# Attention and feed-forward on one core: stage tiles 2080 bytes apart in SBUF instead of 2048

## The chip, the core and the metric

The kernel runs on one NeuronCore of a Trainium2 chip, as one launch. The metric is the device time of that launch in microseconds (us). Engines are named as in the profile: PE is TensorE (PEld its weight loads), DVE is VectorE, ACT is ScalarE, POOL is GpSimd, SP the engine whose queue issues all DMAs.

## The reference

Local-window attention with global tokens, then a feed-forward layer with a leaky ReLU. Eight batches, eight heads, 512 local and 32 global tokens per head, 64 wide. A local token sees the 32 global keys and the local keys at most 32 places away; a global token sees all.

```python
s_g = scale * q_g @ concat(k_g, k_l).T ;  out_g = softmax(s_g) @ concat(v_g, v_l)
s_l = concat(scale * q_l @ k_g.T, where(|i-j| <= 32, scale * q_l @ k_l.T, -1e9))
out_l = softmax(s_l) @ concat(v_g, v_l)
x = concat(out_g, out_l) as [8*544 tokens, 512]
h = x @ w_in                                  # w_in 512 x 2048
g = max(h, 0) + alpha * min(h, 0)             # alpha per column of h
out = g @ w_out                               # w_out 2048 x 512, float32
```

## The kernel before

**Work and order.** The feed-forward layer fills most of the run. Its tokens form nine groups: eight batches of 512 local tokens, and one group of 256 global tokens. In each group a loop over f goes through 16 slices of 128 columns of w_in; one pass of it is called a step T, 144 in all. To keep float32 accuracy each factor is split into a high and a low part in the fp32r type: weights into w_hi and w_lo (tile `wt`), x into `xh` and `xl`, g into `gh` and `gl`. Three products are kept of four.

- `f1(T)` makes h for one slice in PSUM (`h_ps`): for each of four 128-row pieces of x three matmuls, w_hi·xh, w_lo·xh and w_hi·xl, with all tokens of the group (512, or 256 in the last group) as columns of the moving operand: 12 matmuls.
- `leak` (ACT, relu of -h), `bend` (DVE, g = beta·relu(-h) + h), `round_g` (ACT, `gh`), `rest_g` (`gl` = g - gh, on DVE for the first group and on POOL for the others) turn h into g.
- `f2(T - 2)` adds w_out·g to four PSUM banks `o`: eight matmuls with `gh` as moving operand, four with `gl`. After the last slice of a group the banks are copied out (`ost`) and written to HBM.

Every one of these matmuls has its own 128x128 weights, so PE issues one weight load per matmul; the next load runs under the current matmul.

The attention of the 32 pairs of heads is dealt out between these steps. Eight pairs and the decoding of the weights stand ahead in a hand-written order (`ORDER`); the others are planned at fixed steps: `local_scores` (`s_ps`, small matmuls on `qk`), `local_maxima` and `local_exps` (`p`), `local_exchange` (DVE transposes `p` into `pb`, which goes to HBM and comes back as `pt`), `local_values` (`o_ps`), `local_weights` (`xq`, exchanged through `xb` into `x_raw`), and the global tokens' parts (`g_ps`, `gt`, `go`, `gx`). All engine calls go through a recording layer, so DVE, ACT and SP instructions of the opening carry line 77, matmuls line 108, transposes on PE line 111, and `gl` on POOL line 464.

**Where the tiles lie.** SBUF tiles are placed one behind the other, rounded to 32 bytes per partition. The order that matters here: `alpha_sb` (with `PAD[0]` extra columns), `mask`, `ident`, `x_raw`, `x_glb`, `qk` (with `PAD[1]` extra columns), `vw` of the later pairs, small tiles, three wide tiles for the decoding, 21 stage tiles, small tiles, 17 weight tiles of 8192 bytes. The stage tiles hold everything of 512 columns that is short-lived, all under one tag:

```python
def stage(name, dtype=F32):
    return work.tile([128, 512], dtype, tag="st", name=name, bufs=NST)
```

So `xh`, `xl`, `g`, `gh`, `gl`, `p`, `pb`, `pt`, `xq`, `xb` and `ost` are stage tiles. In the built program the 21 of them start at byte 45056, 47104, ... 86016 of each partition, all multiples of 2048; the weight tiles start at 88576 + 8192 n, all multiples of 512. A 128x128 weight slice starts at a multiple of 512 in its tile. The distance from the moving operand of a feed-forward matmul to its weights is therefore a multiple of 512 for all 3456 of them. `x_raw` starts at 384 past a multiple of 512.

Of the kernel before, what the change touches and what calls it, by code (L numbers as in the profile page):

```python
# [27 lines left out]
NST = 21  # L28
# [2 lines left out]
TC = dict(schedule_with_timeline_sim=True)  # L31
HP = 50
HPU = 4
PAD = (32, 32)
LAG = 2
NRAW = 2 * NPAIR
ORDER = """
# [46 lines left out]
def longformer_ffn(ctx: ExitStack, tc: tile.TileContext, qk, vs, gn, vg, w, alpha, out):  # L84
# [5 lines left out]
    work = ctx.enter_context(tc.tile_pool(name="work", bufs=1))  # L90
# [3 lines left out]

    alpha_sb = const.tile([128, NF + PAD[0]], F32, name="alpha_sb")[:, 0:NF]
    mask = const.tile([128, 4, 128], F32, name="mask")
# [14 lines left out]
        return tc.keep_in_program_order(nc.tensor.transpose(*a))  # L111

    def stage(name, dtype=F32):
        return work.tile([128, 512], dtype, tag="st", name=name, bufs=NST)

    def small(name, n=4):
        return work.tile([128, n], F32, tag=name, name=name, bufs=4)
# [93 lines left out]
    def load_qk(P):  # L211
        if P < NPAIR:
            qks[P] = wpool.tile([128, 2048], F32, tag="w", name="qk")[:, 0 : SL + KS]
        else:
            qks[P] = work.tile([128, SL + KS + PAD[1]], F32, tag="qk", name="qk", bufs=1)[:, 0 : SL + KS]
        dma.dma_start(qks[P], qk[P])
# [31 lines left out]
    def local_maxima(P):  # L248
        for h in range(2):
            s, mn = ps_of[P, h], small("mn")  # L250
            if P < NRAW:
                src, scale = s.rearrange("q (i n) -> q i n", i=4), 0.125
                vec.tensor_reduce(mn, src, axis=AX.X, op=ALU.max)
                vec.tensor_scalar(mn, mn, -0.125, None, op0=ALU.mult)
            else:
                p = stage("p")
                src, scale = p.rearrange("q (i n) -> q i n", i=4), -1.0
                vec.scalar_tensor_tensor(p, s, -0.125, mask.rearrange("q i n -> q (i n)"), op0=ALU.mult, op1=ALU.add)
                vec.tensor_reduce(mn, src, axis=AX.X, op=ALU.min)
                pr_of[P, h] = p  # L260
            ps_of[P, h] = src, mn, scale

    def local_exps(P):
        z_of[P] = small("z", 8)
        for h in range(2):
            src, mn, scale = ps_of.pop((P, h))
            p = pr_of[P, h] = stage("p") if P < NRAW else pr_of[P, h]
            for i in range(4):
                k = 2 * i + h
                act.activation(p[:, 128 * i : 128 * i + 128], src[:, i], AF.Exp, bias=mn[:, i : i + 1], scale=scale, accum_out=z_of[P][:, k : k + 1])  # L270
        rz_of[P] = small("rz", 8)
        act.activation(rz_of[P], z_of.pop(P), AF.Copy, bias=1e-9)
# [9 lines left out]
    def local_copies(P):  # L282
        for h in range(2):
            pt_of[P, h] = stage("pt")
            copy("a" if P >= NPAIR or P in (3,) else "d", pt_of[P, h], ps_of.pop((P, h)))
# [368 lines left out]
```

## Time and profile before

| what | us |
|---|---|
| median of two timed runs | 916.97 (916.1 to 917.84) |
| the profiled execution, its own time | 917.19 |
| span of its instructions | 915.4 |
| PE busy (share of the span) | 890.9 (97%) |
| PEld busy | 718.8 (79%) |
| DVE, ACT, POOL busy | 438.6, 388.1, 163.1 |
| mean granted TensorE clock | 0.993 |

A busy time is the union of an engine's instructions. A matmul's own duration in the profile runs to the modelled end of its pipeline, so it is longer than the time from one matmul's start to the next one's; the rate is read from starts. "Idle before" names what the engine waited for; on an engine that is not the bottleneck it costs nothing.

### The profile page before, as it was taken

The numbers are of one execution on the slowest core, as the hardware profiler recorded it, in microseconds if no ns is written. First come the engines' busy times: TensorE is split into PE (matmuls) and PEld (weight loads), VectorE is DVE, ScalarE is ACT, GpSimd is POOL, SyncE is SP. The second block draws the span as 40 slices with busy tenths as digits, with TensorE's granted clock in tenths as the row PEclk, the third lists the DMA queues.
The fourth block names the chain that finished last, engine by engine and source line by source line (L and its number), as shares of the span: only waits on it lengthen the run. The fifth ranks groups of instructions, "written<-read, shape, count | busy, mean of one in ns | idle before, by whom it ended". The sixth has DMA issues, their size and how long they took to land.

```text
span 915.4 us, 21219 instructions
## 1 busy us (share of the span) xinstructions
PE 890.9 (97%) x8696; PEld 718.8 (79%) x8704; DVE 438.6 (48%) x840; ACT 388.1 (42%) x1078; POOL 163.1 (18%) x158
## 2 busy tenths in 40 slices
PE   8889998899999999999999999999999999999997
PEld 4568786677887778777887788777887888888897
DVE  6899995354454444554444444554444323111211
ACT  5787873343343344443343344443343333222322
POOL 3000000112111212121112212121122222222221
PEclk9999999899999999999999999999999999999999
DMA  9994335445545454565546454465545330100000
GB/s 330 379 377 169 102 114 164 155 136 188 190 138 192 158 195 146 182 200 186 175 146 195 163 197 146 164 218 183 175 133 171 119 101 24 46 1 1 22 26 24
DMA packets 139953, 140.33 MB, mean 153 GB/s; under 512 B 9296, under 2 KB 112208, under 8 KB 137808
## 3 DMA queue, kind: packets, MB, share of 16 engines
q1 hardware_dynamic: 139856, 138.98, 45.0%
q8 instruction: 68, 1.11, 0.5%
q14 instruction: 29, 0.24, 0.1%
HBM read 111.16 MB, written 27.79 MB: 152 GB/s over the span
## 4 chain that ended last, share of the span: by engine, by line
PE 90%; DVE 4%; DMA 2%; issue 1%; ACT 1%; SPq 1%; DVEq 0%; ACTq 0%
PE o L108 40%; PE h_ps L108 39%; PE o_ps L108 4%; PE s_ps L108 4%; DVE wt L77 2%; PE go L108 1%; PE g_ps L108 1%; SPq L77 1%; DMA ws<-in_w_dram 1%; DMA pb<-pb 1%; PE gt L111 1%; DVE xl L77 0%; PE pt L111 0%; PE gx L108 0%; ACT p L77 0%
## 5 line engine op out<-in xcount | busy, mean ns | idle before, releaser
L108 PE MATMUL h_ps<-xh,wt 128*128 128x512 f32 (+1 forms) x1152 | 339.9, 378 | 0.0
L464 POOL TENSOR_TENSOR gl<-g,gh 128x512 fp32r<-128x512 f32 (+1 forms) x128 | 155.8, 1217 | 744.6 <-ACT gh L77 689.2
L108 PE MATMUL o<-gh,wt 128*128 128x512 f32 (+1 forms) x1152 | 279.1, 385 | 4.1 <-ACT ost L77 4.1
L108 PEld LDWEIGHTS h_ps<-xh,wt 128*128 128x128 f32 x1152 | 212.2, 188 | 41.8 <-issue 0.6
L108 PEld LDWEIGHTS o<-gh,wt 128*128 128x128 f32 x1152 | 205.5, 189 | 48.8 <-issue 6.8
L77 DVE SCALAR_TENSOR_TENSOR g<-g,beta_sb,h_ps 128x512 f32<-128x512 f32 (+1 forms) x144 | 102.2, 710 | 292.9 <-ACT g L77 289.4
L108 PE MATMUL h_ps<-xl,wt 128*128 128x512 f32 (+1 forms) x576 | 217.9, 378 | 0.0
L77 ACT ACTIVATE g<-h_ps 128x512 f32<-128x512 f32 (+1 forms) x144 | 82.0, 570 | 226.2 <-PE h_ps L108 208.6
L108 PE MATMUL o<-gl,wt 128*128 128x512 f32 (+1 forms) x576 | 151.6, 385 | 0.2 <-DVE gl L77 0.2
L77 ACT CAST gh<-g 128x512 fp32r<-128x512 f32 (+1 forms) x144 | 85.7, 597 | 118.7 <-DVE g L77 96.4
L108 PEld LDWEIGHTS h_ps<-xl,wt 128*128 128x128 f32 x576 | 108.4, 188 | 20.3 <-DVE xl L77 0.3
L108 PEld LDWEIGHTS o<-gl,wt 128*128 128x128 f32 x576 | 103.2, 189 | 23.6 <-issue 4.6
L77 ACT ACTIVATE p<-p,mn 128x128 f32<-128x128 f32 x192 | 74.5, 390 | 104.7 <-DVE mn L77 82.4
L77 DVE STREAM_TRANSPOSE pb<-p 128x512 f32<-128x512 f32 x48 | 34.0, 710 | 25.9 <-ACT p L77 25.6
L77 DVE TENSOR_TENSOR xq<-o_ps,rz 128x512 f32<-128x512 f32 x32 | 22.1, 692 | 42.0 <-PE o_ps L108 33.0
L108 PEld LDWEIGHTS o_ps<-vw,pt 128*32 128x32 f32 x2048 | 30.2, 110 | 15.0 <-issue 6.5
L108 PE MATMUL s_ps<-qk 64*32 64x128 f32 x2048 | 38.5, 278 | 3.1 <-issue 3.1
L108 PE MATMUL o_ps<-vw,pt 128*32 128x64 f32 x2048 | 35.8, 221 | 3.0 <-DMA pt<-pb 2.5
L108 PEld LDWEIGHTS s_ps<-qk 64*32 64x32 f32 x2048 | 29.2, 107 | 10.1 <-issue 7.2
L77 ACT ACTIVATION_READ_ACCUMULATOR p<-p,mn 128x1 f32 x192 | 36.0, 188 | 0.0
L77 DVE TENSOR_TENSOR xl<-x_raw,xh 128x512 fp32r<-128x512 f32 x28 | 21.5, 814 | 20.5 <-ACT xh L77 17.3
L77 DVE SCALAR_TENSOR_TENSOR p<-s_ps,mask 128x512 f32<-128x512 f32 x48 | 30.1, 665 | 1.3 <-PE s_ps L108 1.3
(83 smaller groups left out, 547.0 us busy)
## 6 DMA issues: line engine op xcount, KB each, us to landing
vw<-in_vs_dram SPq DMA_DIRECT2D x64, 512.0 KB, 5.3
qk<-in_qk_dram SPq DMA_DIRECT2D x32, 672.0 KB, 6.5
ws<-in_w_dram SPq DMA_DIRECT2D x16, 1024.0 KB, 9.3
pb<-pb SPq DMA_DIRECT2D x48, 256.0 KB, 2.1
pt<-pb SPq DMA_DIRECT2D x192, 64.0 KB, 1.9
vg<-in_vg_dram SPq DMA_DIRECT2D x32, 320.0 KB, 3.4
gn<-in_gn_dram SPq DMA_DIRECT2D x32, 288.0 KB, 4.4
out_dram<-ost SPq DMA_DIRECT2D x32, 256.0 KB, 2.6
```

The lines of the kernel that those rows point to most:

```text
L77: ins = call(*a, **k)
L108: return tc.keep_in_program_order(nc.tensor.matmul(*a, **k))
L111: return tc.keep_in_program_order(nc.tensor.transpose(*a))
L464: (vec if T < NF else nc.gpsimd).tensor_tensor(gl[:, 0:n], gs.pop(T)[:, 0:n], gh_of[T][:, 0:n].bitcast(F32), op=ALU.subtract)
```

## The change

The tile behind a stage tile gets eight more columns of 4 bytes, and the tile is a view of its first 512. The stage tiles are then 2080 bytes apart. `PAD[1]`, which lengthens the `qk` tile, goes from 32 to 120 columns (352 bytes more); together with 21·32 = 672 bytes of the stage tiles that moves everything behind them by 1024.

```diff
-PAD = (32, 32)
+PAD = (32, 120)
+STEP = 8
...
     def stage(name, dtype=F32):
-        return work.tile([128, 512], dtype, tag="st", name=name, bufs=NST)
+        return work.tile([128, 512 + STEP], dtype, tag="st", name=name, bufs=NST)[:, 0:512]
```

In the built program the stage tiles start at 45408, 47488, ... 87008: 352 past a multiple of 512, and 32 more with each tile, so that each of the 16 multiples of 32 below 512 occurs. The weight tiles start at 89600 + 8192 n, still multiples of 512. The distance from moving operand to weights, taken modulo 512, now has 16 values, each at 124 to 392 of the 3456 feed-forward matmuls. Successive feed-forward matmuls differ in it in 1435 of 3455 places; before, in none. `vw` of the later pairs moves from 256 to 96 past a multiple of 512, the wide tiles from 384 to 224. `qk` and all tiles ahead of it stay. No instruction is added, taken away or moved: on every engine the instructions, their buffers and the semaphores that they wait for stand in the same order in both programs; only line numbers behind the two edits differ by one.

## Prediction

> **What bounds the kernel now.** I read the page's busy times and granted clock first, then the windows by stage, the groups of instructions by form, the timeline of PE, and last the chain of work.
>
> ```profile
> PE 890.9 (97%) x8696; PEld 718.8 (79%) x8704; DVE 438.6 (48%) x840; ACT 388.1 (42%) x1078; POOL 163.1 (18%) x158
> PE 90%; DVE 4%; DMA 2%; issue 1%; ACT 1%; SPq 1%; DVEq 0%; ACTq 0%
> 0.00:50.00 50.00, 39.83 (x698) 24.80 (x706) 37.33 (x63) 34.26 (x108) 7.27 (x30) 0.97 1.00 361
> 50.00:100.00 50.00, 48.79 (x396) 38.58 (x396) 48.06 (x63) 38.45 (x76) 0.00 (x0) 1.00 0.56 214
> 100.00:150.00 50.00, 49.81 (x526) 39.90 (x525) 45.32 (x62) 35.83 (x75) 0.00 (x0) 1.00 0.43 139
> 400.00:450.00 50.00, 50.00 (x559) 39.92 (x558) 23.29 (x55) 18.71 (x59) 10.29 (x8) 1.00 0.51 169
> 800.00:850.00 50.00, 50.00 (x222) 41.40 (x221) 6.73 (x9) 10.96 (x18) 11.73 (x10) 1.00 0.00 1
> ```
>
> PE is busy 97% of the span and makes 90% of the chain of work. The rows by stage (columns: busy us and count of PE, PEld, DVE, ACT, POOL, then clock, DMA share, GB/s) say that outside the opening nothing else comes near: from 400 us on PE has no idle time, the others half or less. Only in the first 150 us are DVE and ACT close (DVE 131 us of 150 in three rows). The clock is full. So the question is what a matmul costs, and that is read from starts:
>
> ```profile
> 810.12 0.62 PE L108 MATMUL h_ps<-xh,wt 128*128 128x512 f32 x2
> 810.35 0.19 PEld L108 LDWEIGHTS h_ps<-xl,wt 128*128 128x128 f32 x1
> 810.57 0.39 PE L108 MATMUL h_ps<-xl,wt 128*128 128x512 f32 x1
> 812.84 0.39 PE L108 MATMUL o<-gh,wt 128*128 128x512 f32 x1
> 894.79 1.12 PE L108 MATMUL o<-gh,wt 128*128 128x256 f32 x8
> 895.75 0.64 PE L108 MATMUL o<-gl,wt 128*128 128x256 f32 x4
> ```
>
> From 810.12 to 812.84 lie twelve matmuls of 512 columns: 2.72/12 = 0.2267 us each. The eight of 256 columns take 0.96/8 = 0.120. The weight load (0.19) starts with a matmul's start and runs under it. These are the groups:
>
> ```profile
> L108 PE MATMUL h_ps<-xh,wt 128*128 128x512 f32 x1024 | 316.2, 390 | 0.0
> L108 PE MATMUL o<-gh,wt 128*128 128x512 f32 x1024 | 261.2, 397 | 4.1 <-ACT ost L77 4.1
> L108 PE MATMUL h_ps<-xl,wt 128*128 128x512 f32 x512 | 199.8, 390 | 0.0
> L108 PE MATMUL o<-gl,wt 128*128 128x512 f32 x512 | 141.3, 398 | 0.2 <-DVE gl L77 0.2
> ```
>
> Together 3072 matmuls of 512 columns, 3072 x 0.2267 = 696 us, and 384 of 256 columns, 46 us: 742 of the span's 915 us. They are exactly the matmuls whose moving operand is a stage tile. One nanosecond more or less on each is 3.1 us.
>
> One more thing in this trace bears on the change. The matmuls do not always keep that rhythm:
>
> ```profile
> 406.85 2.11 PE L108 MATMUL o<-gh,wt 128*128 128x512 f32 x8
> 408.80 1.07 PE L108 MATMUL o<-gl,wt 128*128 128x512 f32 x4
> 418.78 0.40 PE L108 MATMUL o<-gh,wt 128*128 128x512 f32 x1
> 419.94 0.40 PE L108 MATMUL o<-gh,wt 128*128 128x512 f32 x1
> ```
>
> Between the start at 418.78 and that at 419.94, right behind a piece of attention, lie five intervals: 1.16/5 = 0.232 each. And eight behind another piece (406.85 to 408.80) take 1.95, 0.14 more than eight of the settled ones (1.81); most of it falls to the first, whose weights were not loaded yet. So after a disturbance the spacing is some 5 ns longer, and within about ten matmuls it settles at 0.2267. Weight load and moving stream do feel each other, or their timing, in some way.
>
> **The change part by part.** No instruction comes, goes or moves; buffers and waits are the same. Only addresses change. So the sum has one term for each place where an address could set a duration.
>
> (1) The 3072 matmuls of 512 columns. The trace of before has no feed-forward matmul at a distance other than a multiple of 512, so the price has to be bounded. From above: if the new distances keep the rhythm from settling, each interval is 0.232 and not 0.2267, 5 ns more. From below: perhaps distance 0 is what costs. The nearest row is the opening's fillers, which have the same number of columns in bf16 and whose weights are a slice of the very tile that they stream:
>
> ```profile
> 51.16 2.10 PE L108 MATMUL h_ps<-x_glb 128*128 128x512 bf16 x8 [2.80 <-DVE g L77]
> 52.91 0.81 PE L108 MATMUL h_ps<-xh,wt 128*128 128x512 f32 x2
> ```
>
> Eight in 1.75: 0.219 each. If the fp32r ones came down to that, each would save 8 ns. I take +1 ns, close to no change, and the reason is the row at 810. In those twelve matmuls the weights step through distances that differ by 512, 1024 and 1536 bytes, and the spacing does not move by a nanosecond; also, one load walks 512 bytes while the matmul above it walks 2048, so in every pair the two reading places pass through all distances modulo 512, wherever they start. A cost of being at the same place would then be paid once per matmul before and after. What is left is the settling: the distance jumps in 1435 of 3455 places, each a small disturbance that could cost part of 5 ns. A fifth of 5 ns gives +1 ns, 3072 x 1 = **+3 us**; bounds -25 (8 ns) and +15 (5 ns).
>
> (2) The 384 matmuls of 256 columns: the same two bounds in proportion, 3.5% and 2.3% of 46 us, -1.6 and +1.1; taken as 0. Of the attention's matmuls, those of `o_ps` take their weights from a stage tile (`pt`) and stream `vw`, which moves too:
>
> ```profile
> L108 PE MATMUL o_ps<-vw,pt 128*32 128x64 f32 x2048 | 35.8, 221 | 3.0 <-DMA pt<-pb 2.5 <-DVE pt L77 0.3
> ```
>
> They work in slices of 128 and 256 bytes, so they already lie at many distances; 36 us altogether, 1% of it is 0.4 us: 0.
>
> (3) DVE and ACT. Their stage operands now lie at all distances too, and in the first 150 us they are nearly bound. Here the trace has two distances for one operation:
>
> ```profile
> L77 DVE TENSOR_TENSOR xl<-x_raw,xh x28: 678/686/1441, 140.5 to 769.2; 128x512 fp32r<-128x512 f32 x28
> L77 DVE TENSOR_TENSOR gl<-g,gh x16: 648/684/692, 55.3 to 146.8; 128x512 fp32r<-128x512 f32 x16
> ```
>
> The columns after the count are min/median/max in ns. `xl` reads `x_raw` (384 past a multiple of 512) and a stage tile, `gl` two stage tiles at distance 0: medians 686 and 684. I price this at 0. If the cover failed, 1% on the 131 us that DVE works in the first 150 would be at most 1.3 us.
>
> (4) POOL's `gl`, 1286 ns, all at distance 0 today:
>
> ```profile
> L464 POOL TENSOR_TENSOR gl<-g,gh 128x512 fp32r<-128x512 f32 x112 | 144.0, 1286 | 707.6 <-ACT gh L77 661.8 <-issue 39.2 <-DMA pb<-pb 4.3
> 809.84 1.29 POOL L464 TENSOR_TENSOR gl<-g,gh 128x512 fp32r<-128x512 f32 x1 [4.15 <-ACT gh L77]
> ```
>
> It may get shorter or longer; it has 4.15 us of idle time before it in a step of 24 x 0.2267 = 5.44, and its result is wanted two steps later. Even at twice the time PE would not see it: 0.
>
> (5) DMAs into and out of stage tiles now start off the multiples of 256 bytes. Two transfers of the same size and piece length bound that: `pt` lands at multiples of 2048 today, `x_raw` at 384 past a multiple of 512.
>
> ```profile
> pt<-pb SPq DMA_DIRECT2D x192, 64.0 KB, 1.9
> x_raw<-xb SPq DMA_DIRECT2D x96, 64.0 KB, 2.0
> PE o_ps L108 <- DMA pt<-pb: 2.5, 1, 2.5
> ```
>
> 0.1 us later for `pt`, which is issued four steps (22 us) ahead of the matmuls that read it; PE waited for it once, 2.5 us in total. If the one wait repeated: 0.1 us. The opening, where DMA is full (share 1.00), loads weight tiles, which stay at multiples of 512. Price 0.
>
> The sum: the profiled execution's 917.19 (span 915.4 and 1.8 around it) + 3 = 920.2; it stands 0.2 above the median of 916.97, so against that **920 us**, +0.3%. About 2% (18 us) is what a measurement of this kernel tells from no change.
>
> **The rivals.** First, **the rhythm never settles**. For it: the longer spacing after each disturbance, and 1435 jumps. Against: the settling itself survives twelve different weight places. Price: the two upper bounds, 15.4 + 1.1 = +16.5, 933; if the spacing were worse than 0.2327 (6 ns x 3072 = 18 us) it would be slower by over 2%.
>
> Second, slower for sure: **at some distances the weight load cannot run under the matmul**. Place: each pair at such a distance; then the next matmul waits for its weights as the first one does behind attention, where the eight above cost 0.14 more. One distance of sixteen is 3072/16 = 192 matmuls x 0.14 = +27, 944. It decides from 18/0.14 = 130 matmuls, 4% of them. For it: all loads run at one distance today, so nothing shows that others work. Against: `h_ps<-xl` and the others pass four distances modulo 2048 without one such case.
>
> Third, faster: **distance 0 is the bad case**, and 0.2267 holds a collision of the load's first bytes with the stream's. Then nearly all matmuls (all but 172 of 3456) save up to 8 ns: -25 - 1.6, about 891. Half of it would be 904. For it: 0.2267 against 0.219 for the fillers. Against: those fillers are at distance 0 as well, so the difference goes with the data type before it goes with the distance. [...]
>
> That the change does nothing at all to the addresses is excluded: the built program has them.
>
> **How the numbers follow.** My forecast, rhythm as before or nearly so, 0.60, with its own range 914 to 926. Never settling 0.17, of which 0.06 beyond 2%. Loads that do not overlap 0.11, all beyond 2%. Distance 0 the bad case 0.12, of which 0.09 beyond 2%. Faster by over 2%: 0.09. Slower by over 2%: 0.06 + 0.11 = 0.17. Within: 0.74. The range for eight times in ten leaves out the deeper part of the third rival and half of the second: 906 to 940.
>
> **What would show it.** Right: in the windows from 800 to 850 PE still has x222 in 50 us, the groups above keep means of 390 to 398 and LDWEIGHTS 188, the twelve of a settled step take 2.72, and PE is busy 97%. A spacing that never settles shows as x217 or fewer in that window, with DVE, ACT and POOL unchanged. Loads that do not overlap show as single intervals near 0.36 inside a step and as a high max of the matmuls' durations. The third rival shows as x226 or more. Term (3) is wrong if the median of `xl` or `gl` on DVE moves by over 10 ns, (5) if PE's waits for `pt` reach a microsecond per pair. The forecast as a whole is wrong if the spacing in the quiet stretch from 800 us on, where nothing but PE matters, leaves 0.2267 by more than 2 ns in either direction.

## The result, and the profile after

The changed kernel takes 932.14 us (median of two runs, 931.57 to 932.71) against 916.97: 1.016 times as long, 95% interval 1.0128 to 1.0193. It is slower by 15 us. That lies inside the range of the forecast, but not in the likeliest case's own, 914 to 926; it is what the first rival gave (933).

The page of the profile after, the two rows that answer to those of before:

```profile
span 929.8 us, 21227 instructions
PE 905.9 (97%) x8704; PEld 719.8 (77%) x8704; DVE 438.7 (47%) x840; ACT 387.8 (42%) x1078; POOL 163.7 (18%) x158
```

The span is 14.4 us longer and PE is busy 15.0 us longer; DVE, ACT and POOL are busy as long as before to within 0.6 us. PE has the same 97%: it does not wait more, its work has become longer. The windows say where that can be seen best (columns: busy us and count of PE, PEld, DVE, ACT, POOL, then clock, DMA share, GB/s):

```profile
800.00:850.00 50.00, 50.00 (x217) 40.51 (x216) 6.65 (x9) 10.96 (x18) 11.65 (x9) 1.00 0.00 1
```

In the quiet stretch, without attention and nearly without DMA, 217 matmuls stand where 222 stood. A window of 50 us catches every matmul of which a part lies in it, so the count is (50 + 0.39) over the spacing: 222 is 0.227 us, 217 is 0.232. The timeline gives it from starts, first of before, then of after:

```profile
812.84 1.98 PE L108 MATMUL o<-gh,wt 128*128 128x512 f32 x8
818.28 1.98 PE L108 MATMUL o<-gh,wt 128*128 128x512 f32 x8
823.72 1.98 PE L108 MATMUL o<-gh,wt 128*128 128x512 f32 x8
```

```profile
804.66 2.03 PE L109 MATMUL o<-gh,wt 128*128 128x512 f32 x8
810.24 2.03 PE L109 MATMUL o<-gh,wt 128*128 128x512 f32 x8
815.78 2.02 PE L109 MATMUL o<-gh,wt 128*128 128x512 f32 x8
821.34 2.03 PE L109 MATMUL o<-gh,wt 128*128 128x512 f32 x8
826.92 2.03 PE L109 MATMUL o<-gh,wt 128*128 128x512 f32 x8
```

From one group of eight to the next lie the 24 matmuls of a step. Before, a step takes 5.44 us each time, 0.2267 per matmul. After, four steps take 22.26 us, 0.2319 per matmul, and they differ: 5.58, 5.54, 5.56, 5.58. The 256-column matmuls of the last group went the other way:

```profile
905.23 0.40 PE L109 MATMUL h_ps<-xh,wt 128*128 128x256 f32 x2
905.46 0.28 PE L109 MATMUL h_ps<-xl,wt 128*128 128x256 f32 x1
905.58 0.40 PE L109 MATMUL h_ps<-xh,wt 128*128 128x256 f32 x2
906.29 0.40 PE L109 MATMUL h_ps<-xh,wt 128*128 128x256 f32 x2
```

Nine of them from 905.23 to 906.29, 0.118 each; before, 0.120.

So the sum of the difference is 3072 x (0.2319 - 0.2267) = 16.0 us, less 384 x 0.002 = 0.8, makes 15.2, against 14.4 in the span. The first term is a little too large, because matmuls behind attention were spaced wider before already: over the whole run the starts of neighbouring 512-column matmuls, where they are less than 0.3 us apart (some 2880 in each trace), lie 0.2276 us apart before and 0.2323 after, which makes 14.4 and not 16.0. The last microsecond was not located.

### The profile page after: what moved, and what is told of

It is laid out like the page before. It is cut to its first block, busy times and chain, and to the rows that moved or that the text cites. A ratio compares the mean times of both kernels' runs of the same rounds, so it can differ in the third digit from the quotient of the medians.

```text
span 929.8 us, 21227 instructions
## 1 busy us (share of the span) xinstructions
PE 905.9 (97%) x8704; PEld 719.8 (77%) x8704; DVE 438.7 (47%) x840; ACT 387.8 (42%) x1078; POOL 163.7 (18%) x158
## 4 chain that ended last, share of the span: by engine, by line
PE 89%; DMA 5%; DVE 3%; issue 1%; SPq 1%; POOL 0%; ACT 0%; DVEq 0%; POOLq 0%; ACTq 0%
PE o L109 41%; PE h_ps L109 38%; PE s_ps L109 4%; PE o_ps L109 3%; DMA qk<-in_qk_dram 2%; DMA pb<-pb 1%; DMA xb<-xb 1%; DVE wt L78 1%; PE go L109 1%; PE g_ps L109 1%; PE gt L112 1%; SPq L78 1%; DVE mn L78 1%; DVE pt L78 0%; PE gx L109 0%
## 5 line engine op out<-in xcount | busy, mean ns | idle before, releaser
L109 PE MATMUL h_ps<-xh,wt 128*128 128x512 f32 (+1 forms) x1152 | 344.6, 382 | 0.0
L109 PE MATMUL o<-gh,wt 128*128 128x512 f32 (+1 forms) x1152 | 283.7, 388 | 6.1 <-ACT ost L78 4.1
L109 PE MATMUL o<-gl,wt 128*128 128x512 f32 (+1 forms) x576 | 153.7, 389 | 0.0
L78 DVE TENSOR_TENSOR xq<-o_ps,rz 128x512 f32<-128x512 f32 x32 | 22.1, 691 | 42.7 <-PE o_ps L109 33.3
L78 DVE TENSOR_REDUCE mn<-p 128x4 f32<-128x512 f32 x48 | 30.4, 658 | 0.1
```

What stands on the lines that cost most here:

```text
L78: ins = call(*a, **k)
L109: return tc.keep_in_program_order(nc.tensor.matmul(*a, **k))
```

## The experiments

All are the kernel before with tiles placed elsewhere. Unless said otherwise the stage tiles stay 2048 bytes apart and each engine's instructions, their buffers and waits stand in the same order as before. "Starts" below are residues modulo 512 of the moving operands (stage tiles) and of the weights. Two sets of runs of the kernel before stand beside them, with a median of 918.39 for the first four experiments and 919.01 for those behind (914 to 923 over 31 runs); ratios are against these.

**Both moved by 128.** The distance stays 0, the starts do not.

```diff
-PAD = (32, 32)
+PAD = (32, 64)
```

> Stage tiles and weight tiles both start 128 past multiples of 512, 2048 and 8192 apart: distance 0 at all 3456 feed-forward matmuls, but no longer at multiples of 512. Distance theory (the spacing of two matmuls depends on where the moving operand lies relative to the weights): 0.2267 us as before, 917 us. Start theory (it depends on where the moving operand itself starts): 0.233, 936 us. Jump theory (only a distance that changes from matmul to matmul keeps the spacing from settling): 917.

Measured: 920.64 us, ratio 1.0042 (1.0011 to 1.0072).

```profile
800.00:850.00 50.00, 50.00 (x223) 41.40 (x222) 6.73 (x9) 11.44 (x19) 11.60 (x9) 1.00 0.00 1
```

223 matmuls in the quiet stretch: the spacing of before. With both starts at 128 nothing is lost there, which rules out the start theory. The 0.4% are not in the spacing. In the profiled execution PE waits 1.5 us for a copy of results (`ost`) on DVE and 1.7 us for `qk`, two waits that the kernel before does not show; whether they are the cause was not followed up.

**Only the stage tiles moved by 128.** One constant distance, no jumps.

```diff
-PAD = (32, 32)
+PAD = (32, 64)
...
-        m, z = small("gm", 4), small("gz", 16)
+        m, z = small("gm", 4), small("gz", 40)
```

The wider `gz`, behind the stage tiles, brings the weights back to a multiple of 512.

> Stage tiles 128 past multiples of 512 and 2048 apart, weight tiles at multiples of 512: one constant distance of 384 modulo 512, no jumps. Distance theory: spacing 0.2333 settled (the changed kernel's runs of eight at this residue alternate between 229 and 238 ns), 3072 x 6.6 ns = 20 us more than before, some 935 to 937. Start theory: the same 936. Jump theory: 0.2267 settled, 917.

Measured: 936.02 us, ratio 1.0204 (1.0171 to 1.0236).

```profile
800.00:850.00 50.00, 50.00 (x216) 40.20 (x215) 7.82 (x11) 11.64 (x20) 11.20 (x9) 1.00 0.06 21
```

The timeline of the same kernel, from one group of eight to the next but one:

```profile
802.87 2.03 PE L108 MATMUL o<-gh,wt 128*128 128x512 f32 x8
808.47 2.03 PE L108 MATMUL o<-gh,wt 128*128 128x512 f32 x8
814.07 2.03 PE L108 MATMUL o<-gh,wt 128*128 128x512 f32 x8
```

A step takes 5.60 us, 0.2333 per matmul, and now the same each time: the rhythm does settle, at another value. A constant distance without one jump costs more than the whole change. So the loss needs no jumps, and the jump theory, which gave 917 here, falls.

**Only the weights moved by 128.**

```diff
-        m, z = small("gm", 4), small("gz", 16)
+        m, z = small("gm", 4), small("gz", 24)
```

> Stage tiles at multiples of 2048 as before, weight tiles 128 past multiples of 512: constant distance of 128. Distance theory: 0.233, some 936. Start theory (of the moving operand): 917. Jump theory: 917.

Measured: 932.93 us, ratio 1.0184 (1.0155 to 1.0214).

```profile
800.00:850.00 50.00, 50.00 (x217) 40.55 (x216) 6.73 (x9) 10.97 (x18) 11.61 (x9) 1.00 0.02 7
```

Slower by nearly as much, with the stage tiles where they always were. With the first experiment this shows that it is the distance between the two operands, whichever of them moves.

**Stage tiles moved by 256.**

```diff
-PAD = (32, 32)
+PAD = (32, 96)
...
-        m, z = small("gm", 4), small("gz", 16)
+        m, z = small("gm", 4), small("gz", 32)
```

> Stage tiles 256 past multiples of 512, weight tiles at multiples of 512: constant distance of 256. Distance theory with a period of 256, as the changed kernel's runs at this residue suggest (231, 226, 227, 227): 0.2267, 917. Distance theory with a period of 512: over 930. Start theory with a period of 512: 936. Jump theory: 917.

Measured: 917.62 us, ratio 0.9999 (0.9973 to 1.0026).

```profile
800.00:850.00 50.00, 50.00 (x222) 41.42 (x221) 6.73 (x9) 10.99 (x18) 11.61 (x9) 1.00 0.00 1
```

As before: 256 is as good as 0, so the distance counts modulo 256. That holds to about a nanosecond: the two experiments ahead have distances of 128 and 384, which are equal modulo 256, and their spacings are 0.2333 (the stage tiles moved) and 0.232 (the weights moved). Why they differ is not known.

**Stage tiles moved by 64, and by 32.** An unused tile behind the stage tiles fills up to the next multiple of 512.

```diff
-PAD = (32, 32)
+PAD = (32, 48)                                      # 64; (32, 40) for 32
...
+    gap = ctx.enter_context(tc.tile_pool(name="gap", bufs=1))
...
+    gap.tile([128, 112], F32, name="gap_sb")         # 64; 120 columns for 32
```

> Stage tiles 64 past multiples of 512 and 2048 apart, weight tiles at multiples of 512: one constant distance of 448. Distance theory: each residue has a settled spacing of its own, and the changed kernel's runs of eight at this one show 226, 229, 232 in turn, so 0.229: 3072 x 2.3 ns = 7 us more, some 924. Two-class theory (0 modulo 256 good, everything else 0.2333): 936.

> Stage tiles 32 past multiples of 512 and 2048 apart, weight tiles at multiples of 512: the smallest step of the change as a constant distance. Distance theory: the changed kernel's runs of eight at this residue go 230, 235, 233, 234, mean 0.2333: 3072 x 6.6 ns, some 935 to 937. If 32 bytes are too little to matter: 917.

Measured: 64 takes 924.13 us, ratio 1.0054 (1.0033 to 1.0076); 32 takes 935.88, ratio 1.0174 (1.0145 to 1.0203). First the kernel with 64, then that with 32:

```profile
800.00:850.00 50.00, 50.00 (x220) 41.00 (x220) 7.05 (x10) 11.17 (x19) 11.64 (x9) 1.00 0.00 1
```

```profile
800.00:850.00 50.00, 50.00 (x216) 40.15 (x215) 7.30 (x10) 11.13 (x19) 11.08 (x10) 1.00 0.06 21
```

220 is 0.229 and 216 is 0.233. So there are more than two classes: 64 costs a third of what 32 and 128 cost, and the price does not grow with the distance. The smallest step of the change costs in full. In these two the start of the stage tiles moves together with the distance; the two were told apart at 128 alone.

**Jumps between 0 and 256 alone.** The stage tiles 2304 apart; for space there are 18 of them and not 21, which changes the order of the program too.

```diff
-NST = 21
+NST = 18
...
-        return work.tile([128, 512], dtype, tag="st", name=name, bufs=NST)
+        return work.tile([128, 512 + 64], dtype, tag="st", name=name, bufs=NST)[:, 0:512]
```

> Stage tiles 2304 apart (18 of them, for space), weight tiles at multiples of 512: the distance jumps between 0 and 256, the two that settle at 0.2267 when constant. If the jumps themselves cost (the changed kernel's matmuls at these two distances average 231 ns), PE starts x217 or x218 matmuls between 800 and 850 us and the time is 925 to 930. If only the distance counts, x222 and 917, plus what three stage tiles fewer may cost.

Measured: 955.56 us, ratio 1.0391 (1.0374 to 1.0408), and in the quiet stretch:

```profile
800.00:850.00 50.00, 50.00 (x222) 41.38 (x222) 11.19 (x15) 14.39 (x25) 12.20 (x10) 1.00 0.07 24
```

222: jumps between two distances that are equal modulo 256 do nothing to the spacing. The total was not expected: three stage tiles fewer cost some 37 us. The group of the `gh` matmuls shows one place of it, PE idle 22.1 us for copies of the results (4.1 before):

```profile
L108 PE MATMUL o<-gh,wt 128*128 128x512 f32 x1024 | 267.6, 404 | 22.2 <-ACT ost L77 22.1
```

PE's waits for `gn` on ACT are another, 8.8 us (0.4 before), and the granted clock is 0.97 from 600 to 650 us and 0.90 from 700 to 750 (1.00 in both before). So this kernel and the three built on it are read in the quiet stretch only.

**Fillers in bf16 at a distance of 128.** The fillers stream from 128 bytes behind their weights; what they compute is not used.

```diff
+    idle2 = halves[:, 1088:1600]
...
-            matmul(ps, idle[:, 0:128], idle, start=not add, stop=not add)
+            matmul(ps, idle[:, 0:128], idle2, start=not add, stop=not add)
```

> As before, but the bf16 fillers of the opening stream from 128 bytes behind their weights instead of from the same address (what they compute is not used). If distance acts on every matmul of 512 columns: some 6 ns more than 0.216 to 0.219 each. If it acts only where the stream is 4 bytes wide: 0.216 to 0.219 as before. The time as before, 917, either way.

Measured: 919.98 us in one run. The timeline at the eleven fillers ahead of the first transposes, before and in the experiment:

```profile
10.57 2.54 PE L108 MATMUL pt<-x_glb 128*128 128x512 bf16 x11 [0.16 <-issue]
```

```profile
11.07 2.54 PE L108 MATMUL pt<-x_glb 128*128 128x512 bf16 x11 [0.16 <-issue]
```

Both (2.54 - 0.38)/10 = 0.216 us each, the 0.38 being the last one's own duration. A distance of 128 does nothing to these bf16 matmuls of the same 512 columns. The other place of the prediction, the fillers near 51 us, cannot be compared: in the experiment the eight of them take 602 ns each (378 before), where those of the row above take 379 as before, and what slowed them was not followed up.

**Finer distances.** The kernel with 18 stage tiles 2304 apart, each used from its element 1, 4 or 12 on: 4, 16 or 48 bytes past multiples of 256.

```diff
-        return work.tile([128, 512 + 64], dtype, tag="st", name=name, bufs=NST)[:, 0:512]
+        return work.tile([128, 512 + 64], dtype, tag="st", name=name, bufs=NST)[:, 1:513]   # 4:516, 12:524
```

> 18 stage tiles 2304 apart, each used from its second element on: moving operands 4 bytes past multiples of 256, all distances equal modulo 256. Read in the quiet stretch (the whole is some 36 us longer for the three stage tiles that are missing, as with the jumps of 256). If only an exact multiple of 256 settles at 0.2267: x217 or fewer starts from 800 to 850. If what counts is a block of 16 or 32 bytes: x222.

> The same with moving operands 16 bytes past multiples of 256. If what counts is a block of 32 bytes, x222 and 0.2267 in the quiet stretch; if a smaller one, a spacing between 0.2267 and 0.2333 or beyond, x216 to x221.

> The same with moving operands 48 bytes past multiples of 256, between 32 (0.2333) and 64 (0.2289). By blocks of 32 bytes: 0.2333, x216. By a smooth dependence: near 0.231, x218.

Measured, in one run each: 982.05 us for 4 bytes, 965.10 for 16, 965.49 for 48. From 800 to 850 us these three still had attention in progress, so the counts of the expectations do not apply; the 20 us behind are quiet, and there the spacing of before gives (20 + 0.39)/0.2267 = 90. The rows for 4, 16 and 48 bytes:

```profile
850.00:870.00 20.00, 20.00 (x86) 15.88 (x85) 2.92 (x4) 4.28 (x7) 3.88 (x3) 1.00 0.01 1
```

```profile
850.00:870.00 20.00, 20.00 (x88) 16.21 (x87) 2.99 (x4) 4.87 (x8) 4.96 (x4) 1.00 0.00 1
```

```profile
850.00:870.00 20.00, 20.00 (x87) 16.19 (x86) 2.98 (x4) 4.27 (x7) 5.16 (x4) 1.00 0.00 1
```

86, 88 and 87 are 0.237, 0.232 and 0.234; a count of 20 us is good to about 1%. Four bytes are the worst of all that were tried, 16 bytes are not free either, and 48 costs what 32 does: in the kernel with 32 the same 20 us hold 87 too. Blocks of 32 bytes are ruled out by the 16, and a price that rises or falls steadily with the distance is ruled out too. Blocks of 16 are ruled out by the 4 only if it is the distance that acts there; a start that is off by 4 bytes could cost something by itself, and no run separates the two.

No version beat the kernel before. The only gain seen is the 0.002 us of the 256-column matmuls, 0.8 us in all, which could not be told from no change.

## Why the prediction was right and wrong

By its own sign the forecast was wrong: the spacing in the quiet stretch left 0.2267 by 5 ns, and 2 were allowed. The time lies inside the range of 906 to 940 because other cases had been given room there, not because of the case that was chosen.

**What bounds the kernel** was right: PE's spacing set nearly all of the difference, and the terms beside it were close to their prices.

**Term (1)**, the 512-column matmuls, is the step that failed. It was bounded at +15 us by the row of the unsettled spacing, 0.232, and that is what the change cost: 16 by the steps of the timeline. Then the forecast chose +1 ns per matmul, +3 us, with the reason that in every pair the two reading places pass through all distances modulo 512, so that "a cost of being at the same place would then be paid once per matmul before and after". That was the author's estimate from the sizes of the two operands; no trace shows where a load or a stream reads at a given moment. The experiments show that the distance at the start does count: the spacing is 0.2267 at 0 and 256, 0.229 at 64, 0.232 to 0.233 at 32 and 128. The row it leaned on, twelve matmuls whose weights step by 512, could show nothing: 512, 1024 and 1536 are all 0 modulo 256, so it was one case twelve times. That the residues were one class was written down in the part on the tiles; the row should have been read as no evidence, and the choice left nearer the upper bound. That the bound came so close is luck: 0.232 was read at distance 0, from matmuls that had not settled, and the settled spacing at 32 and 128 is 0.2333, beyond it. The bound from below was misread as well. The eight fillers at 51.16 have a first gap of 0.43 us, two intervals with one record missing (a weight load stands at 51.38 without its matmul), so the 1.75 us are not eight intervals; the other starts there lie 0.215 to 0.216 apart, like the fillers at 10.57. The bound would have been 11 ns and -34 us instead of 8 ns and -25.

**The jumps**, which were to carry the rest of the term and the whole first rival, are not needed for the loss. A constant 128 costs 17.6 us over its own runs of the kernel before, and jumps of 256 leave the spacing alone. The rival's time came out and its mechanism did not: the rhythm does settle at other distances, at a longer spacing. Worked out from the residues alone, with 2 of 16 at 0.2267, those at 64 modulo 256 at 0.229 and the others at 0.233 (32 and 128 were measured as constants; 0.233 for the rest is an assumption), the mean of the changed kernel is near 0.232, as measured. But the parts do not agree as the sum does. From 200 us on, the changed kernel's matmuls at 0 modulo 256 are followed by the next after 0.2314 us on average and those at 64 modulo 256 after 0.2313, while in the kernel before, at distance 0 throughout, it is 0.2275, and at a constant 64 the quiet stretch gives 0.229. So a matmul's own distance does not give its spacing alone; whether its neighbours' distances do the rest, and what a jump between unequal distances adds or saves, was not tested by itself.

**Term (2)**: taken as 0, measured -0.8 us, inside its bounds of -1.6 and +1.1, though these came from the 512-column matmuls, which went the other way.

**Terms (3) and (4)** were right. The rows of after (min/median/max in ns):

```profile
L78 DVE TENSOR_TENSOR xl<-x_raw,xh x28: 679/686/1439, 140.0 to 782.2; 128x512 fp32r<-128x512 f32 x28
L78 DVE TENSOR_TENSOR gl<-g,gh x16: 652/684/692, 52.3 to 146.2; 128x512 fp32r<-128x512 f32 x16
L465 POOL TENSOR_TENSOR gl<-g,gh 128x512 fp32r<-128x512 f32 x112 | 144.6, 1291 | 722.0 <-ACT gh L78 598.8 <-issue 42.2 <-PE o L109 34.5
```

The medians on DVE are 686 and 684 as before, POOL's mean is 1291 after 1286, though their operands now lie at all distances. The first `xl` starts at 140.0 after 140.5: the opening, where DVE is nearly the bound, costs nothing, and the last `xl` 13 us later than before: the loss is spread over the steps between.

**Term (5)** was right too:

```profile
pt<-pb SPq DMA_DIRECT2D x192, 64.0 KB, 2.0
PE o_ps L109 <- DMA pt<-pb: 3.2, 1, 3.2
```

`pt` lands 0.1 us later, as the row of `x_raw` had it, and PE's one wait for it grew by 0.7 us.

**The other rivals.** No load was kept from running under its matmul: from 800 to 850 us no two starts lie more than 0.241 us apart, where the second rival needed single intervals near 0.36. And distance 0 is the best case that was found, not the bad one: the argument against the third rival, that the difference between the fillers and 0.2267 goes with the data type first, held at the one other distance tried for bf16, 128. Those fillers take 0.216; the fp32r matmuls of as many columns take 11 ns more at the best distance tried, 0.2267, and 17 more at 128, 0.2333.

**Not settled.** The runs show that the spacing goes with the distance (0.2267 at 0 and 256, 0.2333 at 128), not through what. That the weight load under the matmul has to do with it is the author's guess and was not shown, and nothing here separates the matmul's own weights from the next one's, which lie at the same residue throughout. Why 64 (0.229) is cheaper than 32 and 128 (0.233) stays open as well, and so does what one matmul's distance does to the next one's spacing.

## What to carry to other kernels

Where fp32r matmuls of 512 columns, each with its own weights, follow each other, place moving operands and weights so that their distance is a multiple of 256 bytes (0.2267 us from start to start at 0 and 256 here, 0.229 to 0.237 at the others tried), and check the addresses in the built program after any change of a tile's size: stage tiles moved by 32 bytes cost 1.7% here. When a trace shows no effect of some quantity, check first whether the quantity took more than one value in it, modulo any period that could matter. And read a spacing from starts in a stretch where nothing else happens; a rival theory can give the right time for the wrong reason, and only kernels with one constant distance each told the two apart.

## What the hardware showed that was not expected

Of 512-column fp32r matmuls, each with its own 128x128 weights, the spacing in this kernel goes with the distance between the two operands, and to about a nanosecond with that distance modulo 256 bytes in the two pairs that were measured (0 and 256, 128 and 384): 0.2267 us at 0 and 256, 0.229 at 64, 0.2333 at 128 when the stage tiles move, 0.232 when the weights do, 0.233 at 32, and, from counts good to about 1%, 0.234 at 48, 0.232 at 16, 0.237 at 4 (for distances other than 0, 128 and 256 the start moved too). With 256 columns it is the other way round, 0.120 at distance 0 and 0.118 in the changed kernel. The mean durations of the `xh` matmuls among them go the same way, 283 ns before, 280 in the changed kernel and 281 with the stage tiles at a constant 128; only 4 bytes, with 287, are longer there as well. The bf16 fillers ahead of the first transposes, of 512 columns too, take 0.216 at distance 0 and at 128. Between 0.2267 and 0.2333 lie 6.6 ns; what the matmuls wait for in them no run shows. DVE and POOL operations with two operands in SBUF showed no such dependence: medians on DVE of 684 ns for `gl` at distance 0 and at all distances and of 686 for `xl` before and after, means on POOL of 1286 and 1291.
